# A gated mix of sliding-block attention and a SwiGLU block: gate rows fetched two slots ahead, value sums added ahead of the slot's other work, wo fetched late in the first chunk, V's rows written behind the stacks

## The chip, the cores and the metric

The kernel runs on one core of a Trainium2 chip. The time is device microseconds (us) from the start to the end of one execution. The core has five engines with a queue each: TensorE (PE in the profile; PEld is its weight load), VectorE (DVE), ScalarE (ACT), GpSimd (POOL) and SyncE (SP), which here only issues DMAs. An engine takes its instructions strictly in the order of its queue, and an instruction that waits for a semaphore holds up all that stand behind it.

## The reference

The input x has 2048 rows of 512. Two branches are computed from it and mixed row by row:

```
g = sigmoid((x * gate_w).sum(-1, keepdims=True))
q, k, v = split(x @ wqkv)                      # 32 heads of 16
scores = q k^T / 4, kept where 0 <= i - j < 256
a = (softmax(scores) v) @ wo
b = (silu(x @ w_gate) * (x @ w_up)) @ w_down   # 1792 hidden columns
out = g * a + (1 - g) * b
```

All is float32. To get float32 accuracy from a faster matmul form, the kernel splits each operand into a high part (a cast) and a low part (the source less the cast) and adds three products: high by high, high by low, low by high.

## The kernel before

**Names.** `split` (L63 to L68) makes the two parts: the cast is L65 on ACT or L67 on another engine, the subtraction L68. `xhi` and `xlo` are the parts of x, in four chunks of 512 rows. A group is 4 heads, so there are 8 groups; a block is 128 rows, so there are 16.

**First stage (prologue).** x and the first weights are loaded and split. Q and K of groups 0 and 1 are projected (`proj`), and V of all rows, two blocks at a time (`vproj`, `vproj2`). `put_v` (L393) copies V from PSUM into one of two buffers `vs` on ACT, and after each odd block POOL's queue writes that buffer to `vd` in DRAM (L398, 672 KB). `stack` (L242) copies split Q and K from tile to tile, 12 DMAs of 128 KB on SP per group and half, into the form that the score products read; `fill_rows` (L376) sets the other rows of those tiles on POOL before. Then `stage1` of group 0 runs between the products of V: a score product on PE (L263) and its row maximum on DVE (L265).

**Main loop.** It has 128 slots and one more: slot t is group t // 16, block t % 16. In a slot four heads (`hd` 0 to 3) are gone through. For each there are a `stage1` product of the next group (L263, L265), a `stage2` product of this group (L304) with its exponential on ACT (L306) and its masks on POOL (L308, L311), and three steps of the projections that fill PE (L215: later groups' Q and K, and the SwiGLU block's gate and up products, which go to DRAM as `raws` by L516). Work that is due at a certain head of a certain slot stands in the table `AT`, into which `later` puts it. Every fourth slot (`part` 0) `av` issues the value products (L328) of 512 rows into two PSUM tiles, and `finish` brings them out in steps that the generator `FIN` runs at fixed places: a copy of the second tile on ACT (L339, at part 0, head 1), the sum with the first tile on DVE (L341, for the first 512 rows L343 too, at part 0, head 2), then transposes and the division (L346 to L355), and POOL writes `od`. The first tile is the PSUM buffer `pb` (in the last turn `pa`), which the projections need again.

**Gate and early down weights.** From slot `GATE0` = 110 on, one block of x rows is fetched per slot on SP (`gate_fetch`, L543, into two buffers that lie in `xlo`), and DVE multiplies it by the gate weights and sums (`gate_block`, L546). `gate_place` (L540) loads the gate weights. Nine blocks of `w_down` are fetched into `ev` buffers (`wd_early`) and split on DVE (L67, L68) in the slots from 114 on, at head 2.

**Hand-over.** In slot 128 the first two hidden tiles are made from `raws` (`first_load`, `first_silu` L574, `first_tiles` L578 with `split`). Then the tiles of the attention are released, and the SwiGLU block starts.

**SwiGLU block.** For each chunk c and each of 14 hidden blocks n, `load_kept` fetches gate and up results from `raws` into `got` (two DMAs of 256 KB, L690), ACT takes the SiLU (L704), DVE multiplies (L705), `halved` splits the result into `hh` (ACT, L65) and `hl` (DVE, L68), and `step` adds 12 matmuls (L83 to L85) with the down weights. A hidden tile is split one round after it was made and multiplied one round after that. In chunk 0 the remaining five blocks of `w_down` (fetched at n = 4 to 8) and the four of `wo` (fetched at n = 6, 8, 10, 12) are loaded and split one round later; in chunk 1 and later the attention output is loaded (`load_oc`), split (`attn_split`) and multiplied by `wo` (`attn_out`).

**Queues.** All loads, the stacks and the `raws` writes share SP's queue; `vd` and `od` are written from POOL's.

Of the kernel before, what the change touches and what calls it, by code (L numbers as in the profile page):

```python
# [19 lines left out]
NB = S // P  # L20
# [3 lines left out]
NF = F // P  # L24
# [9 lines left out]
def gated_mix(ctx, tc, xT, xn, w01, wqk, wv, wo, wgu, wd, gw, out):  # L34
# [4 lines left out]
    nc = tc.nc  # L39
# [129 lines left out]
    with ExitStack() as A:  # L169
# [217 lines left out]
        def v_products(b):  # L387
# [2 lines left out]
                    for xt, wt in ((xhi, wvh), (xlo, wvh))] + \  # L390
                   [(xhi[c][:, k, o:o + P], wvl[:, k]) for k in range(NK)]

        def put_v(b, ps):  # L393
            t = vs[b // 2 % 2]
            nc.scalar.copy(t[:, :, b % 2, :68].rearrange("p g (j e) -> p g j e", e=17)[:, :, :, :DH],
                           ps.rearrange("p (g j e) -> p g j e", j=4, e=DH))
            if b % 2:
                nc.gpsimd.dma_start(vd[:, :, b - 1:b + 1].rearrange("g p b e -> p g (b e)"),  # L398
                                    t.rearrange("p g b e -> p g (b e)"))

        def vproj(b):
            return whole(pp, "pb", v_products(b), lambda ps: put_v(b, ps))
# [62 lines left out]
        for hf in range(2):  # L465
            fill_rows(QT[1], 0.0, hf, nc.gpsimd)
            fill_rows(KT[1], -1.0, hf, nc.gpsimd)
        stack(0, 1)
        stack(1, 0)


# [28 lines left out]
        def later(t, hd, *fs):  # L500
            AT.setdefault((t, hd), []).extend(fs)
# [50 lines left out]
        pieces = [h for t in (*QT[0], KT[0][0]) for h in halves_of(t)]  # L552
        pieces += [halves_of(t)[hf] for hf in range(2) for t in (*QT[1], KT[1][0])] + halves_of(KT[0][1])
        GATE0 = g7 - 2
        later(GATE0 - 1, 1, gate_place)
        for b in range(NB):
            later(GATE0 + b - 1, 3, lambda b=b: gate_fetch(b))
            later(GATE0 + b, 3, lambda b=b: gate_block(b))
        for m, t in enumerate((1, 2, 3, 5, 6, 7, 9, 10, 11)):
            wd_early(g7 + t, ORDER[m], pieces[m])  # L560

# [32 lines left out]
        for t in range(G * NB + 1):  # L594
# [6 lines left out]
            for hd in range(4):  # L601
                run(s1, 1)
                if t < g7:
                    run(s2, 1)
                elif hd % 2 == 0:
                    run(s2, 2)
                run(turns[part], 3)
                for f in AT.pop((t, hd), ()):
                    f()
                if (part, hd) in ((0, 2), (1, 1), (2, 1), (3, 1)):  # L610
                    run(FIN, 1)
                if hd == 1 and part == 0:
                    while tops:
                        top = tops.pop()
                        put_max(*top)
                        later(t + 1, 1, lambda top=top: get_max(*top))
                    if t:
                        ag, c = divmod(d - 1, NCH)
                        av(ag, c)
                        FIN = finish(ag, c)  # L620
                        run(FIN, 1)
# [9 lines left out]
    with ExitStack() as B:  # L631
# [11 lines left out]

        def load_wo(k):
            raw = fetch(wo[:, k], raw2())
            return lambda: split(woh[:, k], wol[:, k], raw, *act)


        OC = [t.bitcast(F32) for c in range(2) for t in (xhi[c], xlo[c])]
# [92 lines left out]
        loads = [(c, ORDER[n]) for c, n in seq if n != MADE]  # L742
        for _ in range(3):
            load_kept(*loads.pop(0))
        fresh, waiting, ready = [], [(0, n, *first_halves[n]) for n in range(2)], []
        for c, n in seq:
            f = ORDER[n]
            todo, ready = ready, []
            if c == 0 and 9 <= n + 5 < NF:
                ready.append(load_wd(ORDER[n + 5], pieces[n + 5], raw2(), (nc.vector, nc.gpsimd)))  # L750
            if c == 0 and n >= 6 and n % 2 == 0:
                ready.append(load_wo((n - 6) // 2))
            if n != MADE and loads:
                load_kept(*loads.pop(0))
            fresh.append((c, n, hidden(c, f)))
# [1 line left out]
                f()  # L757
            while len(fresh) > (c > 0 or n > 1):
                waiting.append(halved(*fresh.pop(0)))
            if c == 0 and n >= NF - 4:  # L760
                load_oc(0, n - NF + 4)
            if c and 1 <= n < 5:
                load_oc(c, n - 1)
            if c == 1 and 2 <= n < 8:
                attn_step(0, n - 2)
            if c and n >= 8:
                attn_step(c, n - 8)
            if len(waiting) > 1:
# [38 lines left out]
```

## Time and profile before

| | us |
|---|---|
| median of 3 runs (lowest to highest) | 832.97 (830.72 to 833.89) |
| the profiled execution | 831.44 |
| its span, first to last instruction | 829.7 |
| PE busy in it | 816.6 |
| DVE, ACT, POOL busy in it | 512.3, 448.1, 355.2 |

The profile is of one execution. Its span is 1.7 us shorter than its own time, and its own time 1.5 us shorter than the median. In timeline rows the first number is the start, the second the duration, and a bracket at the end says how long the engine stood idle before the row and what ended the wait. "SPq" is SP's queue at the issue of a DMA. In rows of windows there follow, after the length, the busy time of PE, PEld, DVE, ACT and POOL with their instruction counts, the granted TensorE clock, the DMA share and GB/s.

### The profile page before, as it was taken

What the parts mean: (1) busy time and instruction counts of PE and PEld (TensorE: products, weight loads), DVE (VectorE), ACT (ScalarE), POOL (GpSimd) and SP (SyncE); (2) the same over time, 40 slices, a digit from 0 to 9 for tenths busy, and PEclk for the clock granted to TensorE, in tenths of its full rate; (3) what the DMA queues carried; (4) which work ended last, traced back from release to release, by engine and by line L of the source; (5) the groups of instructions that cost most, each with busy time, mean ns of one, the idle gap of its engine ahead of it and who ended that gap; (6) DMA issues with size and microseconds to landing.
All of it is one profiled execution on the core that took longest, in us unless ns stands there. A gap on an engine that the chain in (4) does not pass through costs nothing.

```text
span 829.7 us, 21564 instructions
## 1 busy us (share of the span) xinstructions
PE 816.6 (98%) x8306; PEld 677.6 (82%) x8306; DVE 512.3 (62%) x1418; ACT 448.1 (54%) x935; POOL 355.2 (43%) x640
## 2 busy tenths in 40 slices
PE   9999999999999999999999999999998999999998
PEld 6798988888888888887888888777876888888886
DVE  5496677677667667676777677646557443443443
ACT  6413666666666656666666666565654533334341
POOL 5812545555646545555555554356614211011020
PEclk9999999999999999999999999999999999999999
DMA  8574525624624643642642652566768644563721
GB/s 291 162 221 129 164 103 150 185 95 138 201 100 119 182 146 93 183 145 87 184 151 100 176 166 98 165 189 199 255 236 291 204 129 150 183 198 102 240 65 51
DMA packets 70582, 133.27 MB, mean 161 GB/s; under 512 B 14288, under 2 KB 19024, under 8 KB 70480
## 3 DMA queue, kind: packets, MB, share of 16 engines
q1 hardware_dynamic: 66512, 118.00, 45.9%
q0 software_dynamic: 3968, 13.90, 4.6%
q8 instruction: 65, 1.06, 0.6%
q14 instruction: 37, 0.30, 0.1%
HBM read 61.08 MB, written 45.61 MB: 129 GB/s over the span
## 4 chain that ended last, share of the span: by engine, by line
PE 86%; DMA 4%; POOL 3%; SPq 2%; DVE 1%; issue 1%; ACT 1%; POOLq 0%; ACTq 0%; DVEq 0%
PE pb L215 22%; PE pa L215 22%; PE pb L328 7%; PE ps L263 6%; PE ps L85 5%; PE ps L83 5%; PE ps L84 5%; PE ps L304 4%; PE pb L85 2%; PE pb L83 2%; PE pb L84 2%; PE ps L328 2%; PE pb L701 1%; PE pa L701 1%; DMA ev<-wv 1%
## 5 line engine op out<-in xcount | busy, mean ns | idle before, releaser
L265 DVE CUSTOM_DVE_ANT_0 ps<-ps,mask 128x384 f32<-128x384 f32 (+2 forms) x512 | 272.0, 539 | 144.1 <-PE ps L263 73.6
L306 ACT ACTIVATE pt<-ps 128x384 f32<-128x384 f32 (+2 forms) x512 | 240.5, 477 | 118.9 <-PE ps L263 58.6
L308 POOL TENSOR_SCALAR_AFFINE_SELECT pt<-pt 128x256 f32<-128x256 f32 x256 | 107.0, 418 | 221.5 <-ACT pt L306 210.5
L263 PE MATMUL ps<-k,q 63*128 63x384 f32 (+2 forms) x512 | 159.4, 330 | 2.9 <-DVE mx L265 1.7
L304 PE MATMUL ps<-q,k 64*128 64x384 f32 (+2 forms) x512 | 161.3, 328 | 0.0
L215 PE MATMUL pb<-xhi,wh 64*128 64x512 f32 x512 | 112.8, 394 | 1.8 <-DVE on L343 1.8
L215 PE MATMUL pb<-xlo,wh 64*128 64x512 f32 x512 | 111.6, 391 | 0.0
L215 PE MATMUL pb<-xhi,wl 64*128 64x512 f32 x512 | 111.5, 392 | 0.0
L215 PE MATMUL pa<-xhi,wh 64*128 64x512 f32 x512 | 110.6, 394 | 0.0
L215 PE MATMUL pa<-xlo,wh 64*128 64x512 f32 x512 | 109.4, 391 | 0.0
L215 PE MATMUL pa<-xhi,wl 64*128 64x512 f32 x512 | 109.2, 391 | 0.0
L263 PEld LDWEIGHTS ps<-k,q 63*128 63x128 f32 x512 | 89.5, 185 | 21.0 <-issue 7.0
L311 POOL TENSOR_SCALAR_AFFINE_SELECT pt<-pt 128x256 f32<-128x256 f32 x224 | 97.7, 436 | 0.0
L304 PEld LDWEIGHTS ps<-q,k 64*128 64x128 f32 x512 | 91.9, 185 | 4.6 <-issue 0.8
L705 DVE TENSOR_TENSOR sg<-got,sg 128x512 f32<-128x512 f32 x50 | 48.4, 969 | 51.6 <-ACT sg L704 48.2
L328 PE MATMUL ps<-pt,vg 64*32 64x320 f32 (+4 forms) x1408 | 75.2, 346 | 0.0
L328 PE MATMUL pb<-pt,vg 64*32 64x320 f32 (+3 forms) x1360 | 74.0, 350 | 0.1
L265 DVE DVE_READ_ACCUMULATOR2_ANT mx<- 128x1 f32 x512 | 72.0, 141 | 0.0
L328 PEld LDWEIGHTS pb<-pt,vg 64*32 64x32 f32 x1360 | 46.4, 106 | 28.2 <-ACT pt L306 9.9
L215 PEld LDWEIGHTS pb<-xhi,wh 64*128 64x128 f32 x512 | 57.2, 185 | 11.0 <-DVE on L343 2.1
L215 PEld LDWEIGHTS pb<-xhi,wl 64*128 64x128 f32 x512 | 57.2, 184 | 7.7
L215 PEld LDWEIGHTS pa<-xhi,wl 64*128 64x128 f32 x512 | 55.4, 184 | 8.2
(162 smaller groups left out, 1567.0 us busy)
## 6 DMA issues: line engine op xcount, KB each, us to landing
raws<-ev SPq DMA_DIRECT2D x104, 256.0 KB
got<-raws SPq DMA_DIRECT2D x100, 256.0 KB
od<-on POOLq DMA_DIRECT2D x32, 256.0 KB, 2.9
raw<-wgu SPq DMA_DIRECT2D x28, 256.0 KB
q<-xhi SPq DMA_DIRECT2D x56, 128.0 KB
k<-xhi SPq DMA_DIRECT2D x56, 128.0 KB
vd<-vs POOLq DMA_DIRECT2D x8, 672.0 KB, 5.0
vg<-vd SPq DMA_DIRECT2D x32, 168.0 KB
```

What stands on the lines that cost most here:

```text
L83: nc.tensor.matmul(ps, lh, rh, start=start and i == 0, stop=False)
L84: nc.tensor.matmul(ps, lh, rl, start=False, stop=False)
L85: nc.tensor.matmul(ps, ll, rh, start=False, stop=stop and i == n - 1)
L215: mm = nc.tensor.matmul(ps[me], w[r], x[r], start=not second and i == 0, stop=bool(second) and i == n - 1)
L263: nc.tensor.matmul(ps[:, :n], QT[g % 2][pr][r, q0:q0 + P], KT[g % 2][pr][r, k0:k0 + n], start=True, stop=True)
L265: mx = nc.vector.tensor_tensor_reduce(out=ps[:, :n], in0=ps[:, :n], in1=mask[:, 3 * P - n:], scale=1.0, scalar=NEG, op0=ALU.add, op1=ALU.m ...
L304: nc.tensor.matmul(ps[:, :n], KT[g % 2][pr][r, k0:k0 + P], QT[g % 2][pr][r, k0:k0 + n], start=True, stop=True)
L306: BEHIND.append(nc.scalar.activation(pt[:, j, :n], ps[:, :n], AF.Exp, scale=SCALE))
L308: nc.gpsimd.affine_select(out=pt[:, :, :P], in_=pt[:, :, :P], pattern=[[0, 2], [1, P]], compare_op=ALU.is_ge, fill=0.0, base=0, channel_mu ...
L311: nc.gpsimd.affine_select(out=pt[:, :, 2 * P:], in_=pt[:, :, 2 * P:], pattern=[[0, 2], [-1, P]], compare_op=ALU.is_ge, fill=0.0, base=-1, ...
L328: nc.tensor.matmul(AV[g, c][h][32 * j:32 * j + 32, q0 - c * CH:q1 - c * CH], VG[4 * g + kb // 4][o, kb % 4, 17 * j:17 * j + 32], PT[g, kb, ...
L705: nc.vector.tensor_tensor(out=sg, in0=gu[1], in1=sg, op=ALU.mult)
```

## The change

There are five edits.

1. `send_v` is taken out of `put_v`; the writes of V's first two pairs of blocks (`send_v(1)`, `send_v(3)`) are issued after `stack(0, 1)` instead of in the middle of the projections. The later writes stay with their copies.
2. The gate weights and the first two blocks of gate rows are fetched at slot 108 (before: 109, and the blocks at 109 and 110); each later block is fetched right behind the sum that frees its buffer, two slots ahead of its use.
3. In a slot, `FIN` runs ahead of the work in `AT`.
4. In chunk 0 the splits of `w_down` go from DVE and POOL to ACT (cast) and DVE (subtraction), those of `wo` from ACT and POOL to ACT and DVE; `wo` is fetched at n = 9 to 12 and split two rounds later.
5. The attention output of chunk 0 is loaded and worked on two rounds later, that of the other chunks too is loaded two rounds later.

```diff
+        def send_v(b):
+            if b % 2:
+                nc.gpsimd.dma_start(vd[:, :, b - 1:b + 1].rearrange("g p b e -> p g (b e)"),
+                                    vs[b // 2 % 2].rearrange("p g b e -> p g (b e)"))
...
-            if b % 2:
-                nc.gpsimd.dma_start(vd[:, :, b - 1:b + 1].rearrange("g p b e -> p g (b e)"),
-                                    t.rearrange("p g b e -> p g (b e)"))
+            if b > 3:
+                send_v(b)
...
         stack(0, 1)
+        send_v(1)
+        send_v(3)
         stack(1, 0)
...
-        later(GATE0 - 1, 1, gate_place)
+        later(GATE0 - 2, 1, gate_place, lambda: gate_fetch(0), lambda: gate_fetch(1))
         for b in range(NB):
-            later(GATE0 + b - 1, 3, lambda b=b: gate_fetch(b))
             later(GATE0 + b, 3, lambda b=b: gate_block(b))
+            if b + 2 < NB:
+                later(GATE0 + b, 3, lambda b=b: gate_fetch(b + 2))
...
                 run(turns[part], 3)
+                if (part, hd) in ((0, 2), (1, 1), (2, 1), (3, 1)):
+                    run(FIN, 1)
                 for f in AT.pop((t, hd), ()):
                     f()
-                if (part, hd) in ((0, 2), (1, 1), (2, 1), (3, 1)):
-                    run(FIN, 1)
...
-            return lambda: split(woh[:, k], wol[:, k], raw, *act)
+            return lambda: split(woh[:, k], wol[:, k], raw, nc.scalar, nc.vector)
...
+        FIRST_OC = (0, NF - 1), (1, 0), (1, 1), (1, 2)
+        second = []
...
-            todo, ready = ready, []
+            todo, ready, second = ready, second, []
             if c == 0 and 9 <= n + 5 < NF:
-                ready.append(load_wd(ORDER[n + 5], pieces[n + 5], raw2(), (nc.vector, nc.gpsimd)))
-            if c == 0 and n >= 6 and n % 2 == 0:
-                ready.append(load_wo((n - 6) // 2))
+                ready.append(load_wd(ORDER[n + 5], pieces[n + 5], raw2(), (nc.scalar, nc.vector)))
+            if c == 0 and 9 <= n < 13:
+                second.append(load_wo(n - 9))
...
-            if c == 0 and n >= NF - 4:
-                load_oc(0, n - NF + 4)
-            if c and 1 <= n < 5:
-                load_oc(c, n - 1)
-            if c == 1 and 2 <= n < 8:
-                attn_step(0, n - 2)
+            if (c, n) in FIRST_OC:
+                load_oc(0, FIRST_OC.index((c, n)))
+            if c and 3 <= n < 7:
+                load_oc(c, n - 3)
+            if c == 1 and 4 <= n < 10:
+                attn_step(0, n - 4)
```

The lines behind the edits have other numbers after the change: L398 becomes L395, L513 and L516 become L519 and L522, L540, L543 and L546 become L546, L549 and L552, L578 becomes L585, L705 becomes L712.

Three places show what moves. The first is POOL's queue in the prologue, from the fills of the second half of group 0's stack tiles on, before the change:

```order
L376 MEMSET q_87 128x1024
L376 MEMSET k_88 128x1024
L376 MEMSET k_89 128x1024
L398 DMA vd<-vs_115 128x8x168
L398 DMA vd<-vs_116 128x8x168
L68 TENSOR_TENSOR x10lo<-ev,x10hi 128x512
L376 MEMSET q_346 128x1024
L376 MEMSET q_347 128x1024
```

and after it, eight rows on, behind the last of the fills:

```order
L376 MEMSET k_346 128x1024
L376 MEMSET k_347 128x1024
L395 DMA vd<-vs_115 128x8x168
L395 DMA vd<-vs_116 128x8x168
L395 DMA vd<-vs_115 128x8x168
L395 DMA vd<-vs_116 128x8x168
L68 TENSOR_TENSOR wl<-raw,wh 128x512
```

The first two writes of V have moved behind the low part `x10lo` and eight fills, and stand directly ahead of the third and fourth.

The second place is DVE's queue at the hand-over in slot 128 (`ev` are SiLU results and then hidden tiles, `k_89` their low parts, `on` the value sum), before:

```order
L588 TENSOR_SCALAR igate<-gate 128x16
L578 TENSOR_TENSOR ev<-xhi,ev 128x512
L68 TENSOR_TENSOR k_89<-ev,k_89 128x512
L578 TENSOR_TENSOR ev<-xlo,ev 128x512
L68 TENSOR_TENSOR k_89<-ev,k_89 128x512
L341 TENSOR_TENSOR on<-pa,on 128x512
L346 STREAM_TRANSPOSE on<-on 128x512
```

and after:

```order
L595 TENSOR_SCALAR igate<-gate 128x16
L341 TENSOR_TENSOR on<-pa,on 128x512
L585 TENSOR_TENSOR ev<-xhi,ev 128x512
L68 TENSOR_TENSOR k_89<-ev,k_89 128x512
L585 TENSOR_TENSOR ev<-xlo,ev 128x512
L68 TENSOR_TENSOR k_89<-ev,k_89 128x512
L346 STREAM_TRANSPOSE on<-on 128x512
```

The value sum now stands ahead of the two hidden tiles. At the three earlier turns in the gate slots it moves in the same way ahead of an L67 and L68 of an early down weight.

The third place is ACT's queue in chunk 0, rounds n = 5 to 7 (`raw` are the down weights, `hh` the high part of a hidden tile), after the change:

```order
L711 ACTIVATE sg<-got_10719 128x512
L65 CAST q_344<-raw_10791 128x512
L65 CAST hh<-sg 128x512
L711 ACTIVATE sg<-got_10768 128x512
L65 CAST q_345<-raw_10816 128x512
L65 CAST hh<-sg 128x512
L711 ACTIVATE sg<-got_10793 128x512
L65 CAST k_346<-raw_10843 128x512
L65 CAST hh<-sg 128x512
```

Before it, the casts of down weights stood on DVE at these rounds, and the first cast of `wo` stood on ACT between the SiLU and the `hh` of round 7.

## The prediction

> **What bounds the kernel now.** I read the page first (busy time by engine), then the list of who waited for whom on PE, then the timelines around each of those waits.
>
> ```profile
> PE 816.6 (98%) x8306; PEld 677.6 (82%) x8306; DVE 512.3 (62%) x1418; ACT 448.1 (54%) x935; POOL 355.2 (43%) x640
> ```
>
> PE is busy for 816.6 us of a span of 829.7, and no edit takes a matmul away or adds one. So the change can only win idle time of PE, or add some. The list of waits on PE names what there is to win (total, times, longest):
>
> ```profile
> PE pb L215 <- DVE on L343: 1.8, 1, 1.8
> PE ps L263 <- DVE mx L265: 1.7, 1, 1.7
> ...
> PE ps L83 <- ACT hh L65: 1.3, 1, 1.3
> PE ps L263 <- DMA k<-xhi: 1.2, 1, 1.2
> PE ps L85 <- DVE hl L68: 1.0, 2, 0.7
> ```
>
> These five are single events at five places; the rest of PE's 13.1 us of idle time is at the start and in the tail, where nothing is edited. The two last waits of the SwiGLU block (1.3 and 1.0) lie in one window, given next with one of PE's full windows:
>
> ```profile
> 620.00:640.00 20.00, 17.52 (x73) 13.21 (x72) 16.99 (x20) 9.19 (x16) 11.83 (x8) 1.00 0.90 302
> 640.00:660.00 20.00, 20.00 (x90) 16.55 (x89) 7.32 (x12) 10.30 (x18) 3.37 (x3) 1.00 0.73 231
> ```
>
> By the first row PE is idle 2.48 us there. By the second, 90 matmuls take 20 us, so a step of 12 takes 2.67. All that can be won is 1.2 + 1.7 + 1.8 + 2.5 = 7.2 us, 0.9% of the time.
>
> **Part 1, V's writes behind the stacks.** Rows of POOL, SP, PE and ACT in the prologue, the landing of a `k` stack DMA from the chain of work, and the landing times of all eight `vd` writes:
>
> ```profile
> 27.62 1.96 POOL L398 DMA_DIRECT2D vd<-vs  x2
> 36.89 1.84 POOL L376 MEMSET k<- 128x1024 f32 x2
> 50.55 0.89 POOL L398 DMA_DIRECT2D vd<-vs  x1 [2.40 <-ACT vs L395]
> 29.20 1.68 SPq L247 DMA_DIRECT2D q<-xlo  x1
> ...
> 34.61 1.07 SPq L248 DMA_DIRECT2D k<-xhi  x1
> ...
> 37.63 0.59 SPq L248 DMA_DIRECT2D k<-xhi  x1
> 37.63 2.62 DMA k<-xhi
> 40.49 0.33 PE L263 MATMUL ps<-k,q 63*128 63x128 f32 x2 [1.23 <-DMA k<-xhi]
> 45.88 1.07 ACT L395 COPY vs<-pb 128x512 f32<-128x512 f32 x2 [9.57 <-PE pb L215]
> 49.17 1.08 ACT L395 COPY vs<-pa 128x512 f32<-128x512 f32 x2 [2.22 <-PE pa L215]
> DMA to landing us min/median/max: 4.2/5.0/8.0
> ```
>
> POOL sends two `vd` writes at 27.62, and from 29.20 four stack DMAs (5th to 8th of 12) take until 35.68, 6.5 us, where the undisturbed ones go out every 0.64 (0.59 and a gap). That is 3.9 us lost. The twelfth, issued at 37.63, lands at 40.25, and PE waits for it, 1.23 us. With the writes gone from there it is issued at about 33.7 and lands at 36.4, ahead of the 39.26 at which PE wants it. What is late next is PE itself, then DVE's row maxima, which follow PE. **Gain 1.23 us**; the bounds are 0 and 1.23.
>
> The moved writes are issued when POOL's last fill ends, 38.73, about 11 us later, beside the second and third stack. They slow those by the same 3.9 us; the second is read first by the row maxima of the second half, the third in the main loop, so this costs nothing. What could cost is the buffer: ACT's next copy into `vs` (45.88, with the gain 44.65) must wait until the first write has landed. Two writes sent together here land at most 8.0 us after issue, the first by the median of 5.0: 43.7, or 46.7 at worst. PE needs these PSUM buffers again when its next turn ends (the row at 49.17, less 1.23: 47.9), and the two copies take 1.07, so ACT may start as late as 46.9. I take nothing, and keep 1 us as the upper bound.
>
> [...] The write at 50.55 took 0.89 us of POOL while DVE ran row maxima without a gap, no longer than the 0.98 each at 27.62. [...]
>
> **Part 2, gate rows.** POOL's `wl` ends at 528.08, which frees SP:
>
> ```profile
> 517.56 3.80 SPq L516 DMA_DIRECT2D raws<-ev  x3
> 528.10 0.33 SPq L73 DMA_DIRECT2D raw<-wgu  x1
> 529.43 1.04 SPq L543 DMA_DIRECT2D xlo<-xn  x2
> 534.89 0.69 DVE L546 SCALAR_TENSOR_TENSOR xhi<-xlo,xhi 128x512 f32<-128x512 f32 x1 [2.12 <-DMA vg<-vd]
> ```
>
> SP stands from 521.4 to 528.1 at `raw<-wgu`, and the gate rows are queued behind. They go out at 529.43, among other loads, and DVE waits 2.12 us for them in front of the row maxima, which costs PE 1.71. After the change the gate weights and two blocks stand ahead of the third of the `raws` writes at 517.56, so they go out some 8 us earlier. With the 5.15 us of a load under full traffic (a row in part 4) they have landed by about 527. **Gain 1.71 us** (bounds: 0, if DVE is late again behind the 0.69 of the sum, and 1.71).
>
> The change adds a wait here: each later fetch stands on SP behind the sum of the same slot. Behind it are `raws` writes, early down weights and `vg` loads. Where DVE waits for a down weight (until 553.15, below), SP is now held too, until split and sum are done (0.43 + 0.69 + 0.69), about 555. PE needs none of these loads within the turn, and the `raws` writes only have to free one of five `ev` buffers in time, so I cost it at nothing. If that cover fails, the price is the 1.8 us of one such hold.
>
> **Part 3, value sums first.** Rows of ACT, DVE and PE at slot 116:
>
> ```profile
> 553.15 0.43 DVE L67 CAST q<-ev 128x512 fp32r<-128x512 f32 x1 [6.24 <-DMA ev<-wd]
> ...
> 557.48 0.54 ACT L339 COPY on<-ps 128x448 f32<-128x448 f32 x1 [2.16 <-PE ps L328]
> 558.23 0.61 DVE L67 CAST q<-ev 128x512 fp32r<-128x512 f32 x1
> ...
> 560.29 0.61 DVE L341 TENSOR_TENSOR on<-pb,on 128x448 f32<-128x448 f32 x1
> ...
> 561.09 0.50 PE L215 MATMUL pb<-xhi,wh 64*128 64x512 f32 x2 [1.75 <-DVE on L343]
> ```
>
> The copy that L341 needs is done at 558.02, but DVE does the split of a down weight first (558.23 to 560.29). PE wanted `pb` at 559.34. With the sum first, L341 and L343 (560.29 to the 561.09 of PE, 0.8 together) are done at about 559.0. **Gain 1.75 us** (bounds 1.4 and 1.75, as DVE has little to spare).
>
> The same edit costs at the hand-over, slot 128. Rows of DVE, ACT, the chain, SP and PE:
>
> ```profile
> 603.94 0.69 DVE L578 TENSOR_TENSOR ev<-xhi,ev 128x512 f32<-128x512 f32 x1 [2.07 <-ACT ev L574]
> 604.79 0.59 ACT L339 COPY on<-ps 128x512 f32<-128x512 f32 x1
> 605.27 0.63 ACT L65 CAST k<-ev 128x512 fp32r<-128x512 f32 x1
> 608.40 1.96 DMA raws<-ev
> 610.45 4.18 SPq L690 DMA_DIRECT2D got<-raws  x8
> 613.24 0.63 ACT L704 ACTIVATE sg<-got 128x512 f32<-128x512 f32 x1 [2.18 <-DMA got<-raws]
> 615.57 0.50 PE L85 MATMUL ps<-q,hl 128*128 128x512 f32 x1
> ```
>
> L578 ran at 603.94; now L341 stands ahead of it and waits for the copy that ends at 605.38. L341 takes to 606.05, L578 to 606.70, and only then can ACT cast (605.27 before): 1.43 us later. Behind that cast on ACT stands a second one and the last copy of a projection, whose `raws` write (608.40) landed at 610.36 and released the first `got` loads at 610.45. So the loads start 1.43 later, and with them the SiLU at 613.24, `hh`, `hl` and the matmul at 615.57, which already ran without any slack. **Cost 1.43 us**; 0 if another event than that write releases the loads.
>
> **Part 4, the splits of chunk 0.** The chain, the timelines of ACT, DVE and PE, and the grouped row of L705 between 613 and 645:
>
> ```profile
> 614.67 5.15 DMA raw<-wd
> 620.69 0.39 PE L83 MATMUL ps<-k,hh 128*128 128x512 f32 x1
> 632.97 0.62 ACT L65 CAST woh<-raw 128x512 fp32r<-128x512 f32 x1 [4.84 <-DMA raw<-wo]
> 634.14 1.36 DVE L68 TENSOR_TENSOR hl<-sg,hh 128x512 fp32r<-128x512 f32 x1 [2.01 <-ACT hh L65]
> L705 DVE TENSOR_TENSOR sg<-got,sg 128x512 f32<-128x512 f32 x11 | 11.9, 1082 | 3.5 <-DMA got<-raws 3.5
> ```
>
> ACT waits 4.84 us for `wo` at 632.97 with `hh` behind it, and `hl` at 634.14 is slowed to 1.36; PE's 2.48 us follow from such waits. Fetched late and split two rounds later, `wo` has 5.3 us to land. And with no subtraction left on POOL, L705 should fall from a mean of 1.08 us to the 0.69 that L578 takes above. A round is then 0.63 + 0.6 + 0.62 = 1.85 us on ACT and 3 x 0.69 = 2.07 on DVE, under the 2.67 of PE. **Gain 2.48 us.**
>
> Against it stands the first down weight. It landed at 619.82, 9.37 us after the loads began, and its cast now sits on ACT ahead of the `hh` of step 4. Cast 0.62, `hh` 0.6, the subtraction and `hl` on DVE: `hl` is there 11.35 us after the loads began, and PE wants it at 10.69 (620.69 less 610.45, and two matmuls). **Cost 0.7 us.** The next four arrive in time, as the rounds now run faster than PE.
>
> **Part 5** moves loads and products of the attention output inside chunk 1, for which the list has no wait of PE. I cost it at nothing; the loads come away from the 302 GB/s of the window above.
>
> **Sum.** -1.23 - 1.71 - 1.75 + 1.43 - 2.48 + 0.7 = **-5.0 us**. Against the profiled execution's 831.44 this is 826.4. That execution was 1.53 us faster than the median, so for a median I take 832.97 - 5.0 = **828.0 us**.
>
> **The rivals.**
> - **The hand-over costs nothing**: the `got` loads wait for many semaphores, and their releaser is inferred. For it: DVE's and POOL's last work on the old tiles ends about then too. Against it: the chain goes through that write. Then 828.0 - 1.4 = 826.6. Chance 0.20.
> - **ACT waits for every down weight**: five times the 0.7 instead of one, 2.8 more, 830.8. For it: the DMA share is 0.90 in that window; against it: fewer bytes are due there than before. Chance 0.17.
> - **The gate and value-sum edits don't do what they say**: DVE is held by down weights (6.24 us) at the same places, and the 1.71 and 1.75 return as other waits. The gain is 1.5, 831.4. Chance 0.08.
> - **Slower: the moved V writes land late**, starved on POOL's queue or behind the stacks. From 46.9 us on each us late is one on PE. At twice the longest landing, 16 us, the first lands at 54.7; PE loses 7.8 and keeps 3.8 of the gains, 837.0. The decisive point is a landing of 12 us. Against it: 8.0 is the longest seen. Chance 0.05.
>
> **How the numbers follow.** My forecast has a chance of 0.50. A measurement here tells about 0.5% (4.2 us) from no change, so faster means below 828.8. The forecast, taken with 1.3 us either way, gives 0.35 of faster and 0.15 of same; the first rival 0.19 and 0.01; the second 0.02 and 0.15; the third 0.08 of same; the last 0.04 of slower and 0.01 of same. That is 0.56, 0.40 and 0.04. The range reaches from the first rival less the spread of the runs, 825.3, to the second, 831.0; outside lie most of the third and fourth rival and the tails.
>
> **What would show it.** On PE's list of waits, L263 for `k<-xhi`, L263 for `mx` and L215 for L343 are gone; the wait for `hl` at step 2 of chunk 0 is new, about 1.4 us, and one at step 4. The first `got` load follows the end of the last L339 by about 6.5 us instead of 5.1 (610.45 less 605.38). L705's mean is near 0.69. No copy into `vs` waits for a `vd` write. I am wrong if new waits on PE appear before 600 us, or if chunk 0 still shows more than 3 us of idle PE.

## The result and the profile after

| | before | after |
|---|---|---|
| median of 4 runs (lowest to highest), us | 833.43 (830.72 to 835.00) | 826.17 (825.25 to 826.54) |
| ratio, 95% interval | | 0.9915 (0.9887 to 0.9943) |
| the profiled execution | 831.44 | 825.82 |
| its span | 829.7 | 824.1 |

The median before now has a fourth run, of 835.00 us, beside the three named above. The kernel is 7.3 us faster by the medians and 5.6 us faster between the two profiled executions. Of the 54 further runs of the kernel before that were timed beside the experiments, two took 1147.59 and 1633.11 us and are left out everywhere. First the page of the changed kernel, busy time by engine:

```profile
PE 815.9 (99%) x8306; PEld 677.6 (82%) x8306; DVE 509.8 (62%) x1422; ACT 451.6 (55%) x940; POOL 343.1 (42%) x631
```

Then the list of waits on PE (total, times, longest):

```profile
PE ps L83 <- ACT hh L65: 0.8, 1, 0.8
PE pb L328 <- ACT ev L519: 0.7, 2, 0.4
PE ps L85 <- DVE hl L68: 0.5, 1, 0.5
```

The three waits named for parts 1 to 3 (L263 for `k<-xhi`, L263 for `mx`, L215 for L343) are gone. Of the new ones, those for `hh` and `hl` are both at step 2 of chunk 0, and those of L328 are at two of the value products. PE's idle time falls from 13.1 to 8.2 us, so 4.9, and its busy time by 0.7. Busy time is therefore not the whole measure. A finer one is to take the same matmul in both traces and subtract its start times:

| matmul | before, us | after, us | difference | change since the row above |
|---|---|---|---|---|
| value products before the gate sums | 521.48 | 520.25 | -1.23 | -1.23 |
| value products after the first gate sums | 539.74 | 536.53 | -3.21 | -1.98 |
| value products ahead of slot 116's sum | 555.37 | 552.16 | -3.21 | 0 |
| next value products | 572.25 | 567.81 | -4.44 | -1.23 |
| next value products | 587.83 | 583.73 | -4.10 | +0.34 |
| first product of step 0, chunk 0 | 609.53 | 605.42 | -4.11 | -0.01 |
| fourth product of step 2 | 615.90 | 613.34 | -2.56 | +1.55 |
| fourth product of step 4 | 621.38 | 619.40 | -1.98 | +0.58 |
| first product of step 12 | 646.13 | 640.50 | -5.63 | -3.65 |
| last product | 825.43 | 819.79 | -5.64 | -0.01 |

The table shows where the 5.6 us come from: V's writes 1.23, the gate rows 1.98, the value sum 1.23 and then -0.34, chunk 0 3.65, and 2.13 are paid at the hand-over and at the first down weight. The value sum's wait of 1.75 is gone, but the two matmuls that the table takes next are those at which PE now waits for ACT's copies (0.45 at 567.81, 0.29 at 583.73).

Timelines of the prologue, SP, PE and ACT, after the change:

```profile
33.61 0.60 SPq L248 DMA_DIRECT2D k<-xhi  x1
39.28 0.22 PE L263 MATMUL ps<-k,q 63*128 63x128 f32 x2
45.09 1.08 ACT L400 COPY vs<-pb 128x512 f32<-128x512 f32 x2 [8.62 <-DMA vd<-vs]
```

The twelfth stack DMA goes out at 33.61, and L263 runs at 39.28 without a bracket, that is without a wait. The copy into `vs` did wait for the first moved `vd` write, until 45.09, but PE needed the buffer only by 46.9. Timelines of DVE at the first gate row and at slot 116:

```profile
531.40 0.69 DVE L552 SCALAR_TENSOR_TENSOR xhi<-xlo,xhi 128x512 f32<-128x512 f32 x1
554.85 0.63 DVE L341 TENSOR_TENSOR on<-pb,on 128x448 f32<-128x448 f32 x1 [0.56 <-ACT on L339]
557.80 0.43 DVE L67 CAST q<-ev 128x512 fp32r<-128x512 f32 x1 [2.20 <-DMA ev<-wd]
```

The gate sum no longer waits, and the value sum waits for its copy alone. The third down weight, which was in time before, now keeps DVE waiting 2.20 us, but only behind the sum. The hand-over and chunk 0, timelines of ACT, SP and PE:

```profile
600.69 0.59 ACT L339 COPY on<-ps 128x512 f32<-128x512 f32 x1
602.64 0.62 ACT L65 CAST k<-ev 128x512 fp32r<-128x512 f32 x1 [1.36 <-DVE ev L585]
607.78 3.91 SPq L697 DMA_DIRECT2D got<-raws  x8
611.80 0.50 PE L83 MATMUL ps<-q,hh 128*128 128x512 f32 x1 [0.78 <-ACT hh L65]
613.01 0.50 PE L85 MATMUL ps<-q,hl 128*128 128x512 f32 x1 [0.47 <-DVE hl L68]
617.07 0.62 ACT L65 CAST q<-raw 128x512 fp32r<-128x512 f32 x1 [1.87 <-DMA raw<-wd]
```

The first `got` load follows the end of L339 (601.28) by 6.5 us, and step 2 waits for `hh` and `hl`. The first down weight's cast waits on ACT, ahead of the `hh` of step 4. The two windows that were shown of before:

```profile
620.00:640.00 20.00, 20.00 (x90) 16.57 (x89) 16.35 (x26) 13.98 (x26) 0.00 (x0) 1.00 1.01 358
640.00:660.00 20.00, 20.00 (x90) 16.54 (x90) 7.92 (x10) 10.07 (x17) 2.57 (x2) 1.00 0.49 158
```

Past step 4, PE issues 90 matmuls per 20 us, its full pace.

### The profile page after: what moved, and what is told of

Read it like the earlier page. It is cut to its first block, busy times and chain, and to the rows that moved or that the text cites. A ratio compares the mean times of both kernels' runs of the same rounds, so it can differ in the third digit from the quotient of the medians.

```text
span 824.1 us, 21565 instructions
## 1 busy us (share of the span) xinstructions
PE 815.9 (99%) x8306; PEld 677.6 (82%) x8306; DVE 509.8 (62%) x1422; ACT 451.6 (55%) x940; POOL 343.1 (42%) x631
## 4 chain that ended last, share of the span: by engine, by line
PE 88%; DMA 4%; POOL 3%; DVE 2%; SPq 1%; ACT 1%; issue 1%; ACTq 0%; POOLq 0%
PE pb L215 22%; PE pa L215 22%; PE pb L328 7%; PE ps L263 6%; PE ps L85 6%; PE ps L84 6%; PE ps L83 6%; PE ps L304 4%; PE pb L84 2%; PE pb L85 2%; PE pb L83 2%; PE ps L328 2%; DMA ev<-wd 1%; PE pb L708 1%; PE pa L708 1%
## 5 line engine op out<-in xcount | busy, mean ns | idle before, releaser
L308 POOL TENSOR_SCALAR_AFFINE_SELECT pt<-pt 128x256 f32<-128x256 f32 x256 | 108.2, 423 | 212.5 <-ACT pt L306 204.0
L263 PE MATMUL ps<-k,q 63*128 63x384 f32 (+2 forms) x512 | 158.6, 330 | 0.0
L215 PE MATMUL pb<-xhi,wh 64*128 64x512 f32 x512 | 115.2, 394 | 0.0
L215 PE MATMUL pb<-xlo,wh 64*128 64x512 f32 x512 | 114.0, 391 | 0.0
L215 PE MATMUL pb<-xhi,wl 64*128 64x512 f32 x512 | 113.8, 392 | 0.0
L215 PE MATMUL pa<-xhi,wh 64*128 64x512 f32 x512 | 112.3, 393 | 0.0
L215 PE MATMUL pa<-xlo,wh 64*128 64x512 f32 x512 | 110.9, 391 | 0.0
L215 PE MATMUL pa<-xhi,wl 64*128 64x512 f32 x512 | 110.7, 391 | 0.0
L263 PEld LDWEIGHTS ps<-k,q 63*128 63x128 f32 x512 | 88.8, 185 | 16.1 <-issue 5.4
L311 POOL TENSOR_SCALAR_AFFINE_SELECT pt<-pt 128x256 f32<-128x256 f32 x224 | 98.7, 441 | 0.0
L712 DVE TENSOR_TENSOR sg<-got,sg 128x512 f32<-128x512 f32 x50 | 44.5, 889 | 51.4 <-ACT sg L711 48.1
L328 PE MATMUL ps<-pt,vg 64*32 64x320 f32 (+4 forms) x1408 | 75.2, 346 | 0.0
L328 PE MATMUL pb<-pt,vg 64*32 64x320 f32 (+3 forms) x1360 | 74.0, 350 | 0.8 <-ACT ev L519 0.7
L328 PEld LDWEIGHTS pb<-pt,vg 64*32 64x32 f32 x1360 | 46.5, 106 | 29.1 <-ACT pt L306 9.9
L215 PEld LDWEIGHTS pb<-xhi,wh 64*128 64x128 f32 x512 | 59.3, 185 | 8.6 <-ACT ev L519 0.3
L215 PEld LDWEIGHTS pb<-xhi,wl 64*128 64x128 f32 x512 | 59.3, 184 | 7.5
L215 PEld LDWEIGHTS pa<-xhi,wl 64*128 64x128 f32 x512 | 56.7, 184 | 7.9
```

Of the source, the lines that this page charges most:

```text
L215: mm = nc.tensor.matmul(ps[me], w[r], x[r], start=not second and i == 0, stop=bool(second) and i == n - 1)
L263: nc.tensor.matmul(ps[:, :n], QT[g % 2][pr][r, q0:q0 + P], KT[g % 2][pr][r, k0:k0 + n], start=True, stop=True)
L308: nc.gpsimd.affine_select(out=pt[:, :, :P], in_=pt[:, :, :P], pattern=[[0, 2], [1, P]], compare_op=ALU.is_ge, fill=0.0, base=0, channel_mu ...
L311: nc.gpsimd.affine_select(out=pt[:, :, 2 * P:], in_=pt[:, :, 2 * P:], pattern=[[0, 2], [-1, P]], compare_op=ALU.is_ge, fill=0.0, base=-1, ...
L328: nc.tensor.matmul(AV[g, c][h][32 * j:32 * j + 32, q0 - c * CH:q1 - c * CH], VG[4 * g + kb // 4][o, kb % 4, 17 * j:17 * j + 32], PT[g, kb, ...
L712: nc.vector.tensor_tensor(out=sg, in0=gu[1], in1=sg, op=ALU.mult)
```

## The experiments

All were timed beside the kernel before, in three sets: e1 to e4, e5 to e8, and e9 to e12. The changed kernel itself was timed in another set. The kernel before has medians of 833.26, 831.8 and 832.54 us in these three, so a difference of about 1 us between sets says little. Below, "clock" is the mean granted TensorE clock of a run. "Behind" and "ahead" of a kernel are by matched matmuls, as in the table above.

| run | median, us (range, runs) | ratio to before (95%) | span of the profiled run |
|---|---|---|---|
| e1 | 824.29 (823.83 to 824.97, 4) | 0.9909 (0.9886 to 0.9931) | 822.1 |
| e2 | 825.45 (825.15 to 825.67, 4) | 0.9922 (0.9900 to 0.9944) | 824.0 |
| e3 | 829.81 (828.56 to 832.52, 10) | 0.9964 (0.9946 to 0.9981) | 827.9 |
| e4 | 827.15 (826.62 to 830.50, 10) | 0.9940 (0.9923 to 0.9958) | 828.8 |
| e5 | 825.28 (824.17 to 826.08, 4) | 0.9908 (0.9873 to 0.9942) | 824.1 |
| e6 | 826.36 (826.19 to 827.13, 5) | 0.9919 (0.9894 to 0.9945) | 825.4 |
| e7 | 827.37 (826.69 to 828.04, 6) | 0.9939 (0.9918 to 0.9960) | 825.5 |
| e8 | 825.72 (824.86 to 826.47, 6) | 0.9919 (0.9895 to 0.9943) | 823.9 |
| e9 | 835.66 (one run) | | 833.9 |
| e10 | 831.35 (829.17 to 832.00, 12) | 0.9981 (0.9964 to 0.9998) | 830.2 |
| e11 | 824.86 (823.64 to 825.47, 6) | 0.9901 (0.9877 to 0.9924) | 823.0 |
| e12 | 833.33 (827.57 to 837.64, 12) | 1.0002 (0.9977 to 1.0027) | 830.0 |

### e1, the value sum behind in the last slot

```diff
+                fin = (part, hd) in ((0, 2), (1, 1), (2, 1), (3, 1))
-                if (part, hd) in ((0, 2), (1, 1), (2, 1), (3, 1)):
+                if fin and t < G * NB:
                     run(FIN, 1)
                 for f in AT.pop((t, hd), ()):
                     f()
+                if fin and t == G * NB:
+                    run(FIN, 1)
```

> The changed kernel with one difference: in slot 128 alone the value sum (L341) stands behind the first hidden tiles again; in all other slots it stays ahead. Theory: that sum ahead of the tile made ACT's cast, the raws write and so the first got load 1.43 us late, and PE lost 1.55 us at step 2 of chunk 0 (matched matmuls of the two traces). Expected span 824.1 - 1.4 = 822.7 us, the first got load about 5.1 us after the end of the last L339 instead of 6.5. Rival: the got loads are released by DVE's last work on the attention's tiles, which now ends later; then the load does not come earlier and the span is 824.1 or more. The wait for hl at step 4 (0.6 us of PE) should stay in both.

Timelines of ACT and SP in e1:

```profile
599.88 0.59 ACT L339 COPY on<-ps 128x512 f32<-128x512 f32 x1
600.36 0.63 ACT L65 CAST k<-ev 128x512 fp32r<-128x512 f32 x1
605.52 4.30 SPq L700 DMA_DIRECT2D got<-raws  x8
```

The cast follows L339 at once, and the loads start 5.05 us after L339's end (600.47), as in the kernel before. The same matmul of step 0 starts 0.81 earlier than in the changed kernel, that of step 12 1.96 earlier, so the hand-over gave 1.15 of the 1.4 expected. The other 0.81 was won near 567 and 583, where this execution did not have the waits of L328 for L519, though nothing was changed there. So those waits differ between executions, whatever else sets them. The rival, that DVE's last work on the old tiles holds the loads, falls for this order. All four runs of e1 lie below all four of the changed kernel, and also below all four of e2, which has the changed kernel's order at the hand-over and ran in the same set. The ratios to the kernel before, 0.9909 and 0.9915 for the changed kernel, can't be told apart; by the traces and by e2, e1 is the better version.

### e2 and e12, the fetch of gate rows half a slot later

```diff
-                later(GATE0 + b, 3, lambda b=b: gate_fetch(b + 2))
+                later(GATE0 + b + 1, 1, lambda b=b: gate_fetch(b + 2))
```

e12 has the value sums behind the other work too, as in e3 below.

> The changed kernel with one difference: the fetch of gate block b + 2 is issued at head 1 of the slot after the sum of block b, instead of right behind that sum at head 3 of the same slot. Theory: in the changed kernel SP stands at that fetch until DVE has done the sum, DVE stands at a down weight, and the next down weight stands behind the fetch on SP; so the ev buffers come free late, and PE waits for ACT's copies (L519) at the value products, 0.85 us by matched matmuls near 567 and 583 us. Expected: those waits go, span 824.1 - 0.85 = 823.25 us. Rival: SP is held by the weights' loads and the raws writes at the same places, or the waits come from the value sum that now stands ahead of the down weight's split; then 824.1.

> The changed kernel with the value sums behind the slot's other work (as in e3) and the gate fetches half a slot later (as in e2). In e3 PE lost 5.4 us near 560 us, since DVE waited 2.73 us for the third down weight, which SP had issued behind a gate fetch that stood until 551.5 us. Theory: without that hold the third down weight lands before DVE wants it, and PE loses 1.5 to 3 us there instead of 5.4: span 827.9 - 2.7 = 825.2 us. Rival: the third down weight is late for another reason (its buffer, or the traffic); then the span is 827.9.

In e2 the waits of L328 are not on PE's list; but e1 lacked them without this edit, so nothing follows from it. SP in e12:

```profile
549.14 0.38 SPq L291 DMA_DIRECT2D vg<-vd  x1
552.21 0.33 SPq L549 DMA_DIRECT2D xlo<-xn  x1
552.59 0.42 SPq L73 DMA_DIRECT2D ev<-wd  x1
```

SP runs ahead of the other engines, reaches the fetch at 549.52 and stands there until 552.21 all the same: half a slot in the program's order took no hold away. In e12 PE waits 3.2 us for L343, and the times are the worst and the widest of all, 827.57 to 837.64. Both runs failed to test what they were made for. But e4, below, has the fetches as before and so no such hold, with the sums ahead. First SP in the changed kernel, the first down weight, the fetch that is held, and the third down weight:

```profile
547.14 0.44 SPq L73 DMA_DIRECT2D ev<-wd  x1
551.84 0.33 SPq L549 DMA_DIRECT2D xlo<-xn  x1
552.69 0.43 SPq L73 DMA_DIRECT2D ev<-wd  x1
```

then the first and the third in e4, and DVE's cast of the third:

```profile
550.89 0.44 SPq L73 DMA_DIRECT2D ev<-wd  x1
553.27 0.42 SPq L73 DMA_DIRECT2D ev<-wd  x1
559.67 0.42 DVE L67 CAST q<-ev 128x512 fp32r<-128x512 f32 x1
```

PE runs 3.7 us behind the changed kernel there, and the first issue is as much later. With the hold the third is issued 5.55 us after the first, without it 2.38, as in the kernel before (550.37 and 552.75), and DVE does not wait for it. So the hold does make the third down weight late.

### e3 and e4, the third and the second edit undone

```diff
+                for f in AT.pop((t, hd), ()):
+                    f()
                 if (part, hd) in ((0, 2), (1, 1), (2, 1), (3, 1)):
                     run(FIN, 1)
-                for f in AT.pop((t, hd), ()):
-                    f()
```

> The changed kernel with the third edit undone: the value sums stand behind the slot's other work in all slots. Theory: PE loses the 1.75 us at slot 116 (L215 for L343) again and wins the 1.43 us at the hand-over: span 824.1 + 1.75 - 1.43 = 824.4 us. If the new waits for ACT's copies (0.85 us) come from this edit, they go too: 823.6. Rival: with the gate rows early, DVE is no longer late at slot 116, and only the hand-over shows: 822.7.

In e4 `gate_place` and `gate_fetch` are the lines of before.

> The changed kernel with the second edit undone: gate weights at slot 109, each block one slot ahead. Theory: DVE waits for gate rows near 533 us again and PE loses 1.98 us (matched matmuls) there, and the new waits for ACT's copies (0.85 us) go, since no fetch stands behind a sum of its own slot: span 824.1 + 1.98 - 0.85 = 825.2 us. Rival: those waits stem from the value sums put first, and stay: 826.1.

Both lost more than expected: e3 3.8 us of span instead of 0.3, e4 4.7 instead of 1.1. In e3 the hand-over gave its gain back as foreseen (1.2), but near 560 PE lost 5.56 us against the changed kernel where 1.75 was expected. DVE's timeline in e3:

```profile
556.71 1.24 DVE L67 CAST q<-ev 128x512 fp32r<-128x512 f32 x1 [2.73 <-DMA ev<-wd]
```

its list of waits on PE:

```profile
PE pb L215 <- DVE on L343: 3.6, 1, 3.6
```

and its windows there, in which the third number from the end is the granted clock:

```profile
558.00:560.00 2.00, 0.52 (x2) 0.50 (x4) 2.00 (x6) 0.00 (x0) 1.02 (x2) 0.55 0.38 146
560.00:562.00 2.00, 2.00 (x12) 1.55 (x10) 1.82 (x7) 0.00 (x0) 0.00 (x0) 0.50 0.43 105
562.00:564.00 2.00, 2.00 (x12) 1.62 (x12) 0.00 (x0) 0.87 (x2) 0.18 (x1) 0.50 1.01 348
564.00:566.00 2.00, 2.00 (x17) 1.61 (x16) 0.85 (x2) 0.57 (x2) 0.59 (x2) 0.75 0.86 319
566.00:568.00 2.00, 2.00 (x22) 1.72 (x20) 1.97 (x6) 1.17 (x3) 1.14 (x2) 1.00 0.10 29
```

Two things add up. The third down weight is late (2.73), and with the old order the value sum waits behind it. And after the idle time the granted clock stands at 0.50: 12 matmuls in 2 us instead of 22. From 560 on PE counts as busy all that time. A mean of 0.55 in the first window and 0.75 in the fourth put the half clock at 558.2 to 565.0, 6.8 us. In e4 it is the same at the gate rows, by PE's timeline:

```profile
535.13 0.58 PE L263 MATMUL ps<-k,q 63*128 63x384 f32 x1 [2.04 <-DVE mx L265]
```

and by windows of 0.5 us:

```profile
535.00:535.50 0.50, 0.37 (x3) 0.37 (x5) 0.50 (x5) 0.00 (x0) 0.00 (x0) 0.77 0.01 4
535.50:536.00 0.50, 0.50 (x6) 0.50 (x6) 0.50 (x3) 0.21 (x2) 0.00 (x0) 0.50 1.00 66
...
538.50:539.00 0.50, 0.50 (x6) 0.46 (x6) 0.22 (x3) 0.15 (x1) 0.00 (x0) 0.82 0.34 131
539.00:539.50 0.50, 0.50 (x8) 0.42 (x6) 0.00 (x0) 0.50 (x2) 0.00 (x0) 1.00 0.00 0
```

A mean of 0.77 is half speed for the last 0.23 us of its window, one of 0.82 for the first 0.18. So the clock is half from 535.27 to 538.68, 3.41 us, which costs half of that, 1.7. With 2.04 of idle time that is 3.7 of the 3.9 by which PE falls behind the changed kernel there. The ten runs of e4 fall in two groups: seven at 826.62 to 827.31 with a clock of 0.999 or 1.000, three at 829.33 to 830.50 with 0.996 to 0.998. The profiled one belongs to the three and has a second such stretch at 617. The seven, mean 827.0, lie 0.8 above the changed kernel and 1.6 above e2 of the same set; 1.1 was expected. Neither theory nor rival had the clock.

### e5 and e6, one half of the fourth edit each

```diff
-                ready.append(load_wd(ORDER[n + 5], pieces[n + 5], raw2(), (nc.scalar, nc.vector)))
+                ready.append(load_wd(ORDER[n + 5], pieces[n + 5], raw2(), (nc.vector, nc.gpsimd)))
```

is e5; in e6 `load_wo` and its place are those of before.

> The changed kernel, but the five down weights of chunk 0 are split on DVE (cast) and POOL (subtraction) as before; wo stays late and on ACT and DVE. Theory: of the 3.7 us that PE gained in chunk 0 most came from ACT no longer waiting 4.84 us for wo; the subtractions on POOL slow L712 from 0.69 us to over 1 us again, which costs at most the last 1.1 us of that gain (matched matmuls at steps 8 to 10), and the 0.6 us that PE waits at step 4 for ACT's first cast goes: span 823.5 to 824.6 us. Rival: the slowed L712 carries the gain; then PE loses 2.5 us or more, 826 us or more.

> The changed kernel, but wo is fetched at n = 6, 8, 10, 12 and split one round later on ACT and POOL as before; the down weights stay on ACT and DVE. Theory: ACT waits for wo with hh behind it again, and PE loses most of the 3.7 us: span 826.5 to 827.8 us. Rival: with the down weights' subtractions off POOL the rounds have enough slack to take the wait: 824.1 to 825.

The grouped row of L712 in e5, from 605 to 645 us:

```profile
L712 DVE TENSOR_TENSOR sg<-got,sg 128x512 f32<-128x512 f32 x13 | 14.4, 1106 | 3.7 <-DMA got<-raws 3.4 <-ACT sg L711 0.3
```

The products stay slow, 1.106 us instead of the 0.687 of the changed kernel, and yet PE lost nothing: past step 6 it stands 0.5 better against the changed kernel than at step 0, since the wait at step 4 is gone. So the late `wo` is enough for the whole gain of chunk 0. In e6 PE lost 1.03 us against the changed kernel between steps 0 and 12 and not 2.5 or more, which lies between theory and rival: with the subtractions off POOL most of the wait for `wo` is absorbed. Each half alone wins most of the 3.65 us; they don't add.

### e7 and e8, the first and the fifth edit undone

> The changed kernel with the first edit undone: the first two writes of V go out in the middle of the projections. Theory: PE waits for the k stack again, 1.30 us by matched matmuls, and nothing later takes that up: span 825.4 us. Rival: a later wait for a transfer, such as for the gate rows or the down weights, takes up the shift: 824.1.

> The changed kernel with the fifth edit undone: the attention output of chunk 0 is loaded and worked on two rounds earlier, that of the others loaded two rounds earlier. Theory: no wait of PE hangs on these loads, nothing changes: span 824.1 us. Rival: its loads now fall beside the wo loads and the got loads at the end of chunk 0, and PE waits for a split there: more than 825.

e7 runs 1.2 us above the changed kernel, as expected, and 1.65 above e8 of the same set, but its trace does not show why: in that execution the first loads of x came late, PE was 1.09 behind at 13.28, and the stack then was in time. The traces of e9 and e10, which have the writes as before too, show waits of L263 for `k<-xhi` of 1.4 and 1.5 us. All traces together show the effect: at the score product at 39.28, the nine experiments with the first edit lie within 0.6 us of the changed kernel, and the kernel before, e9 and e10 1.1 to 1.5 us behind it. e8 changes nothing (span 823.9).

### e9, the kernel before once more

> The kernel before, unchanged, for a second trace. Its runs spread over 829.3 to 835.6 us, those of the changed kernel over 825.25 to 826.54. Theory: the spread lies in two waits that hang on when a load lands, DVE for gate rows (PE lost 1.98 us by matched matmuls near 533 us) and DVE for a down weight ahead of the value sum (1.75 us near 560 us). Expected: these two differ from the first trace by over 0.5 us in sum and make up most of the difference in span, the other stages agree within 0.5 us each. Rival: the spread lies in the prologue or in chunk 0; then the difference shows there.

This execution is 4.2 us longer than the first. By matched matmuls the start gives 0.3, the gate rows -0.05, the value sum 1.79, chunk 0 2.1. PE's wait at the value sum, by its timeline:

```profile
561.64 0.71 PE L215 MATMUL pb<-xhi,wh 64*128 64x512 f32 x2 [2.08 <-DVE on L343]
```

and the windows around it:

```profile
560.00:562.00 2.00, 0.36 (x2) 0.36 (x4) 1.97 (x5) 0.87 (x3) 2.00 (x3) 0.94 0.74 249
562.00:564.00 2.00, 2.00 (x12) 1.54 (x12) 1.44 (x4) 0.00 (x0) 1.22 (x3) 0.50 0.44 107
564.00:566.00 2.00, 2.00 (x16) 1.67 (x14) 1.16 (x4) 0.87 (x2) 0.10 (x1) 0.71 0.96 308
```

The wait is only 0.33 longer than in the first trace (1.75), but here the clock halves, and there it did not; the last section shows what differs. Theory and rival were each half right: the value sum and chunk 0 vary, the gate rows did not.

### e10, the second and third edit alone

> The kernel before with the second and third edit alone (gate rows two slots ahead, value sums ahead); V's writes, the splits of chunk 0 and the attention output as before. Theory: by the first traces it gains 1.98 + 1.75, and loses 1.55 at the hand-over and up to 0.85 at ACT's copies: span 829.7 - 1.3 to 2.2, so 827.5 to 828.4 us, 829.2 to 830.1 with what lies around the span, and since the waits of varying length are gone, its runs lie within 2 us of each other where those of the kernel before cover 6. Rival: the spread has another place; then the runs cover 4 us or more.

The median is 831.35, above the 829.2 to 830.1 expected, and the runs cover 2.8 us, between theory and rival; six of the twelve still have a clock below 0.999. By the trace, up to the first step of chunk 0 PE is 3.28 us ahead of the kernel before; at step 12 it is 0.44 behind it. Timelines of ACT and PE in chunk 0:

```profile
631.99 0.62 ACT L65 CAST woh<-raw 128x512 fp32r<-128x512 f32 x1 [5.59 <-DMA raw<-wo]
633.18 0.50 PE L83 MATMUL ps<-k,hh 128*128 128x512 f32 x1 [2.09 <-ACT hh L65]
```

and a window behind them:

```profile
636.00:638.00 2.00, 2.00 (x7) 1.57 (x6) 1.60 (x2) 1.22 (x3) 1.28 (x1) 0.58 0.81 226
```

The late hand-over costs 1.6 by step 4, and then ACT's wait for `wo`, which PE feels 2.09 us long, and a halved clock take the rest. In this execution, what the gate rows and sums win is given back in chunk 0, where the splits are the old ones.

### e11, the last copy early

```diff
-                        later(t0, 2 * m, lambda m=m: nc.scalar.copy(places[m], ps[m]))
+                        later(t0, 2 * m if t0 < G * NB else 0, lambda m=m: nc.scalar.copy(places[m], ps[m]))
```

with the edits of e1 and e2.

> The changed kernel with three differences: in slot 128 the value sum stands behind the first tiles (as in e1); the fetch of gate rows half a slot later (as in e2); and ACT's last copy of a projection (L519 in slot 128) is moved from head 2 to head 0, ahead of the casts of the first tiles. Theory: that copy's raws write releases the got loads, so they start about 2 us earlier than in e1, and the rest of PE's waits at steps 2 and 4 of chunk 0 goes (0.7 us in e1): span 822.1 - 0.7 = 821.4 us. Rival: the got loads also wait for DVE's last subtraction of the first tiles or for other work in the old tiles; then they don't come earlier, and the span is 822.1.

DVE and SP in e11:

```profile
604.58 0.69 DVE L68 TENSOR_TENSOR k<-ev,k 128x512 fp32r<-128x512 f32 x1 [0.69 <-ACT k L65]
605.45 3.83 SPq L700 DMA_DIRECT2D got<-raws  x8
```

The `raws` write now lands early, and the loads go out when DVE's last subtraction ends (605.27): the rival was right. The hand-over gives 0.25 more than in e1 by the trace, and the time, 824.86, is no better than e1's 824.29 from another set.

## Why the prediction was right, and where it was off

**The bound** held: PE, by the waits it named.

**Part 1** was right: the wait went, the first difference in the table is -1.23 (forecast -1.23). That the two agree to the hundredth is luck, since the starts differ between executions: at 12 us the kernel before was 0.2 us ahead, so the stage itself gave 1.4. One sign was wrong, that no copy into `vs` would wait for a write; it did, until 45.09, inside the slack that the prediction had worked out. POOL's two moved sends, beside the row maxima, took 1.96 us as before, and the first write had landed by 45.09, 6.2 us after its issue, so the rival of late writes fell. That a send could be starved on POOL's queue was not shown: in both traces the two first took 1.96 and each of the other six 0.89 to 0.91.

**Part 2** was right in its mechanism, with 1.98 for 1.71. The step "I cost it at nothing" for SP's new hold was only right because of part 3. The hold, 548.53 to 551.84, makes the third down weight late (DVE waits 2.20 us after, 2.73 in e3), and e3 and e12 show PE's price with the sums behind: 3.2 to 3.6 us of idle time, and a halved clock on top. In the changed kernel there remain the waits of L328, 0.7 us in its trace. They also stand in e5, e6, e7, e10 and e11 (0.4 to 0.9), not in e1, e2 and e8, and in no kernel without the second or the third edit; that the hold causes them was not shown. New waits of PE before 600 us were named as what would prove the forecast wrong; these are such, but small.

**Part 3** was right: the wait of 1.75 went, and the cost of 1.43 at the hand-over came, with the `got` loads 6.5 us behind L339; the table has 1.55, and e1, which undoes that part alone, wins 1.15 of it back. The first rival, no cost at the hand-over, falls.

**Part 4** was mis-sized: "gain 2.48 us" measured 3.65. The 2.48 was idle time. The same quoted row had the better number: 73 matmuls against 90, and 17 at 0.22 us are 3.8. After a wait the first matmul is booked with 0.50 us and the next follows 0.34 behind it (627.51 and 627.85, 634.16 and 634.50 in the kernel before), not the usual 0.23, and this counts as busy. The cost of the first down weight, 0.7, measured 0.58; PE did not wait for the other four, so the second rival falls. That L705 had to become fast was not needed (e5).

**Part 5** was right (e8).

**The sum** for the profiled execution was 826.4, and it took 825.82. That it came so near is in part luck: part 4 gave 1.2 us more and the gate rows 0.3 more than it has, and the new waits of L328, which it does not have, took about 0.8. The forecast of the median, 828.0, is 1.8 us too high, and 1.2 of these come from the last step: "That execution was 1.53 us faster than the median, so for a median I take 832.97 - 5.0". It carries the 1.53 over as if it lay outside the edits, but the changed kernel's median is only 0.35 us above its profiled execution. Of the 52 runs of the kernel before beside these experiments, 26 had a clock of 0.999 or more and a mean of 831.5; the other 26 a mean of 834.1. The profiled run, clock 1.000, is of the first kind. Every one of the 31 timed runs of e1, e2, e6, e7, e8 and e11 had 0.999 or more, and three of four each of the changed kernel and of e5. One stretch of 3.41 us at half clock, 1.7 of some 830 us, lowers the mean of a run by 0.002. So the edits together seem to take away stalls that lower the clock in every second run; only e9's trace shows such a stall of the kernel before directly. Half of 2.6 us is 1.3, which with the 5.6 makes 6.9 of the 7.3 us between the medians.

## What to carry to other kernels

Measure a stall by the matmuls that are missing against a full window, not by idle time, and look at the granted clock behind it: in the trace of e4 a wait of 2.04 us was followed by 3.41 us at half clock, 1.7 us more, and seven of the ten runs of e4 had a clock of 0.999 or more. A wide spread of run times is a reason to look for such a wait: the runs of e12 cover 10 us at clocks of 0.992 to 0.999, those of the kernel before in the same set 8 us at 0.993 to 1.000. The profiled run may not show it, as that of the kernel before did not. Put what waits for data that is always there ahead of what waits for a load; and an order that wins in one stage has to be judged with the slack of the next, as e10 shows.

## What was not expected of the hardware

In these traces the granted clock stood at half after some short stalls of PE. In three stretches that windows of 0.5 us resolve (535 and 617 us in e4, 634 us in e10) it was at 0.50 for 3.41 us each time; in e3 and e12, after waits of 3.6 and 3.2 us, for 6.8 by windows of 2 us, about twice that.

In e4 the four changes of the clock lie at 535.27, 538.68, 617.19 and 620.60, the later three 1, 24 and 25 times 3.413 us behind the first. Cut into pieces of that length, the kernel before around its wait of 1.75 us, and e9 around its wait of 2.08, look like this (the third number from the end is again the clock). The pieces of the kernel before are counted back from 829.38, where its clock goes to 0.50 after the last product, those of e9 from 561.76, where its clock does so behind the wait:

```profile
556.32:559.73 3.41, 3.01 (x64) 2.10 (x46) 3.34 (x6) 2.25 (x6) 3.40 (x7) 1.00 1.05 385
559.73:563.14 3.41, 2.05 (x18) 1.75 (x20) 2.76 (x6) 0.95 (x4) 2.90 (x4) 1.00 0.55 198
```

```profile
558.34:561.76 3.42, 1.34 (x14) 0.85 (x12) 3.39 (x8) 2.53 (x6) 2.65 (x4) 1.00 0.93 334
561.76:565.17 3.41, 3.41 (x18) 2.76 (x20) 2.82 (x7) 0.27 (x1) 1.46 (x3) 0.50 0.59 183
```

In the kernel before, the cut divides the idle time into some 0.40 and 1.36 us, and the clock stays at 1.00. In e9 all 2.08 lie in one piece, and the next has 0.50. The other stalls, cut in the same way, each by its own trace, are like these. The pieces at full clock with 2.04 us (e4), 2.08 (e9), 2.1 (e12) and some 2.4 us (e3, e10) of idle PE were each followed by one at half. In the kernel before and the changed kernel no piece between 8 us and the last product has more than 1.36, and the clock stays at 1.00 there. Between these, 1.65 in e4, in two parts of 0.56 and 1.09, was followed by a piece at half, and 1.66 in e9 (534 to 538 us) was not. The second half of the 6.8 us in e3 and e12 followed a piece that was at half clock itself, with some 1.3 and 1.1 us of idle PE. So a wait of 1.75 us that the cut divides cost no clock, and one of 2.08 that lies in one piece did. That the place of a wait on such pieces is why some runs lose clock and others don't was not shown: in seven of the ten runs of e4 the clock stayed full, but these have no trace.
